# In the second batch, four of eight heads' p·v products as six bfloat16 products each, p split in place in the scores' PSUM bank

## The chip, the cores and the metric

The kernel runs on one core of a Trainium2 chip. The metric is the device time of one execution in microseconds (us). Engines are named as the profile names them: PE is TensorE's matmul, PEld its weight load, DVE is VectorE, ACT is ScalarE, POOL is GpSimd, and SP is SyncE, whose queue issues nearly all DMAs.

## The reference

Four batches, eight heads, 768 positions, head size 40. A recurrence with exponential gates (an mLSTM cell) gives each position a vector per head. The heads side by side are x, 768 x 320, and a token mixer and a channel mixer follow, with residuals:

```python
for t in range(S):
    m_new = np.maximum(f_gate[:, :, t] + m, i_gate[:, :, t])
    f_stab = np.exp(f_gate[:, :, t] + m - m_new)
    i_stab = np.exp(i_gate[:, :, t] - m_new)
    C = f_stab * C + i_stab * einsum('bhd,bhe->bhde', vt, kt)
    n = f_stab * n + i_stab * kt
    h_tilde = einsum('bhde,bhe->bhd', C, qt)
    denom = np.maximum(np.abs(einsum('bhd,bhd->bh', n, qt)), 1.0)
    y[:, :, t] = sigmoid(o_gate) * h_tilde / denom
...
h = relu(x.T @ w_tok1) @ w_tok2;  u = x + h.T
out = u + relu(u @ w_ch1) @ w_ch2
```

## The kernel before, in words

**Units.** The recurrence is computed in chunks: each batch has six units of 128 positions, (b, 0) to (b, 5). For a unit PE makes the scores k·q of the eight heads into two PSUM banks of four heads each (`st_s`, line 312, tile `ps_sc`). DVE multiplies each bank by the decay factors `dd` (`st_p`, line 322) and writes p over `dd` in SBUF. PE multiplies p with v, to which a column of ones is added that gives the denominator (`st_pv`, line 430: 41 columns a head, into the bank `po`). What comes from earlier units is added through a state C (`st_state`: q times C at line 371, the update at lines 379 to 388).

**What a unit needs beforehand.** For the unit after the current one ("n1"), POOL masks `dd` (line 283), ACT takes its exponentials in two groups of four heads (line 293, `prep_exp`) and that of `pq` (line 273), DVE multiplies `q3t` by it (line 279), and POOL scales k (`kw`, line 302). Behind p·v, ACT copies `po` out (`ht`, line 441), POOL multiplies by the sigmoid gate (line 449), DVE makes the denominator (lines 455 to 459), x (line 493) and its rounded part `xh` (line 498), and POOL the rest `xl` (line 500).

**Number formats.** Batches 0 and 1 multiply p and v in float32. Batches 2 and 3 take p and v as three bfloat16 pieces each (`st_pv3`, line 401). The mixers use a high and a low float32r part.

**Order.** There is no planner: each engine runs its instructions in the order in which the code issues them, and waits by semaphores. `att(b)` is a generator of five steps a unit: scores and loads; state; exponentials of n1; p·v and x; the second half of the exponentials and the load of n1's successor's k and v (`kvt`, line 246). The whole attention of batch 1 runs inside the channel mixer of batch 0: its last slots n = 11 to 17 each issue one `gemm1` (line 760, into `ps_h`, with `gh` on ACT, line 765, and `gl` on DVE, line 766) and one `gemm2` (line 679, into `acc`, and line 781 adds the finished sum to x), and advance `att(1)` in between by `STEPS0`. SP issues the loads in the same order: of a unit's loads, `q3t` and `pq` (lines 257 and 265) come a step ahead of `kvt` (line 246), then `dd` and `raw`.

**Buffers that matter.** `kvt` (324 KB a load) has two buffers, `ps_sc` two banks (both are one unit's), the pool `ps_m` two banks, shared by `po`, `pu` and, for the second third of batch 0's channel mixer, its two `acc` sums.

Of the kernel before, what the change touches and what calls it, by code (L numbers as in the profile page):

```python
# [7 lines left out]
F32 = mybir.dt.float32  # L8
# [3 lines left out]
BF16 = mybir.dt.bfloat16  # L12
AF = mybir.ActivationFunctionType
ALU = mybir.AluOpType
# [3 lines left out]
B, H, S, D = 4, 8, 768, 40  # L18
L = 128
NC = S // L  # L20
E1 = D + 1
DM = H * D
# [6 lines left out]
ROW = [h % 3 * 3 + h // 3 for h in range(H)]  # L29
# [5 lines left out]
def kernel(ctx: ExitStack, tc: tile.TileContext, gates, qk, q3, kv, og,  # L35
                            wt1, wt2, wc1, wc2, ident, out):
    nc = tc.nc
# [248 lines left out]
    def prep_exp(u, hf):  # L286
        b, c = u
        dd = T[u]["dd"]
        if b == 0:
            nc.scalar.activation(dd[:, 4 * hf:4 * hf + 4, :], T[u]["phi"][hf], AF.Exp)  # L290
            return
        for h in range(4 * hf, 4 * hf + 4):
            nc.scalar.activation(dd[:, h, :], dd[:, h, :], AF.Exp, bias=bcol[:, c, HP * b + h:HP * b + h + 1])  # L293
# [21 lines left out]

    def st_p(u, mid=iter(())):
        t = T[u]
        for hf in range(2):
            if hf:
                next(mid, None)  # L320
            dd = t["dd"][:, 4 * hf:4 * hf + 4, :]
            nc.vector.tensor_tensor(dd, t["s"][hf], dd, ALU.mult)  # L322

    def three(u):
        return u[0] > 1
# [19 lines left out]
    def prep_v(u):  # L345
        t = T[u]
        vx = t["kv"][:, DM:]
        w = xpool[1].tile([128, 3, H * E1], BF16, tag="v3", name="v3", bufs=1)
        r = ap.tile([128, H * E1], F32, tag="kw", name="vr", bufs=2)
        v = nc.vector  # L350
        v.tensor_copy(w[:, 0], vx)
        v.tensor_tensor(r, vx, w[:, 0], ALU.subtract)
        v.tensor_copy(w[:, 1], r)
        v.tensor_tensor(w[:, 2], r, w[:, 1], ALU.subtract)
        t["v"] = w
# [59 lines left out]
    def st_pv(u, copy=True):  # L415
        b, c = u
        t = T[u]
        vx = t["kv"][:, DM:]
        if "p" in t:
            return st_pv3(u)  # L420
        if c:
            po = t["po"]
        else:
            t["bank"] = ps_m.tile([128, 512], F32, tag="m", name="po")
            po = t["bank"][:, 0:H * E1].rearrange("p (h e) -> p h e", e=E1)
        for h in range(H):
            o, x = po[:, h, :], vx[:, h * E1:(h + 1) * E1]
            if b == 0 and c:
                o, x = po[:, 0:h + 2:h + 1, :], x.unsqueeze(1).to_broadcast([128, 2, E1])
            nc.tensor.matmul(o, t["dd"][:, ROW[h], :], x, start=c == 0 and h == 0, stop=h == H - 1)  # L430
        if b == 0 and c:
            po = po[:, 1:1 + H]
        t["po"] = po
        if b:
            st_ht(u)
# [81 lines left out]
    def att(b):  # L517
        for c in range(NC):
            u = (b, c)
            n1, n2 = after(u, 1), after(u, 2)  # L520
            th = three(u)
            if b + 1 < B and c in (3, 4):
                load_sig(b + 1, c - 3)
            if b > 1 and c == 0:
                sigmoid(b)
            st_s(u)
            if n2 and not three(u):
                load_phi(n2)
            if n1 and not three(u):
                prep_mask(n1)  # L530
            if n2:
                load_qk(n2, 0)
            if th:
                prep_p2(u)
            yield
            if th:
                prep_p3(u)
            else:
                st_state(u)
            if n1 and three(u):  # L540
                prep_mask(n1)
            yield
            if n1:
                prep_exp(n1, 0)
                if not three(n1):
                    prep_q3(n1)
                    prep_kw(n1)
            if n2:
                load_qk(n2, 1)
                if not th:  # L550
                    load_q3(n2)
            yield
            st_pv(u)
            st_hs(u)
            if not th:
                st_x(u)
            yield
            if n1 and three(n1):
                prep_v(n1)
            if th:  # L560
                st_x(u)
            if n1:
                if three(n1):
                    prep_q3(n1)
                    prep_kw(n1)
                prep_exp(n1, 1)
            if n2:
                load_kv(n2)
                if th:
                    load_q3(n2)  # L570
                    load_phi(n2)
            yield
# [212 lines left out]
    def step(g, n=1):  # L785
        for _ in range(n):
            next(g, None)
# [148 lines left out]
    for b in range(B):  # L936
# [61 lines left out]
        for n, (k, p) in enumerate(slots):  # L998
            if b == 0 and 2 < n < 11:
                step(dec_ops(9), 9)  # L1000
            g = gemm1(b, k, p, 0 if b or k == 2 else 1 if n < 2 else 2 - 2 * k)
            if b == 0:
                if n < 3:
                    dec_hi()
                    dec_abs(nxt[2] + 2, both=True)
                    dec_low()
                    step(dec_ops(9, whole=True), 9)
                if n == 2:
                    for _ in range(2):
                        dec_hi(1)  # L1010
                        dec_abs(nxt[1] + 1)
                    dec_low()
                if n == 10:
                    split_x(0, 4)
                    split_x(0, 5)
                if n == 11:
                    phase_t(0, 4, ss)
                    phase_t(0, 5, ss)
                    gemm2(*pend)
                    pend = None  # L1020
                    wx[0].release()
                    wq.release()
                    xpool[1] = ctx.enter_context(tc.tile_pool(name="xp", bufs=1, side="right"))
                    step(ag)
                if n < 11:
                    if n > 2:
                        dec_abs(nxt[2] + 2)
                        dec_hi()
                        dec_low()
                    if n > 8:  # L1030
                        sigmoid(1, (n - 9,))
                    if n in (0, 4, 6, 7, 8):
                        step(pf)
# [68 lines left out]
```

## Time and profile before

| what | value |
|---|---|
| three timed runs | 433.81 us median (433.14 to 434.11) |
| the profiled execution | 433.04 us, its span 431.3 us |
| PE busy in the span | 424.0 us (98%) |
| PEld, DVE, ACT, POOL busy | 407.1, 292.6, 185.0, 141.8 us |
| granted TensorE clock | full in all 40 slices |
| batch 1's attention | 102 to 148 us of the span |

Busy times of different engines lie beside each other. The span is what the profiler sees; the execution's own time is 1.7 us more. In rows of a timeline the first number is the start and the second the length of the instruction or run of instructions, in us; [..] at the end is idle time of the engine just before, and whom it waited for.

### The profile page before, as it was taken

How to read it: one execution, taken by the hardware profiler on the slowest of the kernel's cores; microseconds unless marked ns; L12 is line 12 of the kernel's file. 1: busy time of each engine (PE TensorE's matmuls, PEld its weight loads, DVE VectorE, ACT ScalarE, POOL GpSimd, SP SyncE). 2: the span in 40 equal slices, each digit the busy share in tenths (PEclk: the TensorE clock that was granted, in tenths of full speed). 3: DMA queues.
4: the chain of work that ended last, by engine and by line, in shares of the span. 5: the costliest groups of instructions: out<-in, count | busy, mean ns of one | idle time of the engine just before them, and what ended most of it. 6: DMA issues, size and time to landing. Idle time of an engine off the chain costs nothing.

```text
span 431.3 us, 9384 instructions
## 1 busy us (share of the span) xinstructions
PE 424.0 (98%) x3696; PEld 407.1 (94%) x3697; DVE 292.6 (68%) x650; ACT 185.0 (43%) x426; POOL 141.8 (33%) x186
## 2 busy tenths in 40 slices
PE   7999999999999999999999999999999999999996
PEld 3888999999999999999999999999999999999996
DVE  7989877745776788688795688688885645323212
ACT  5987666894544725324414336234334112211111
POOL 7487485860553410341330330331440110000000
PEclk9999999999999999999999999999999999999999
DMA  7997759813878612145356121343240000000000
GB/s 211 287 278 241 247 143 340 251 37 112 236 209 231 205 56 83 64 130 151 92 172 193 59 70 32 127 129 105 90 114 32 2 17 15 2 32 0 26 7 30
DMA packets 24576, 52.37 MB, mean 121 GB/s; under 512 B 2565, under 2 KB 13325, under 8 KB 24533
## 3 DMA queue, kind: packets, MB, share of 16 engines
q1 hardware_dynamic: 24293, 51.61, 39.1%
q8 instruction: 29, 0.48, 0.5%
q10 hardware_dynamic: 240, 0.18, 0.2%
q14 instruction: 14, 0.11, 0.1%
HBM read 47.73 MB, written 4.04 MB: 120 GB/s over the span
## 4 chain that ended last, share of the span: by engine, by line
PE 86%; DMA 5%; POOL 2%; DVE 2%; ACT 2%; issue 1%; SPq 0%; POOLq 0%; ACTq 0%
PE ps_h L760 30%; PE acc L679 28%; PE ps_a L679 5%; PE ps_sc L312 5%; PE ps_b L679 5%; PE po L430 4%; PE po L401 3%; PE pu L379 3%; DMA wst<-in_wt_dram 2%; DMA wst<-in_wc_dram 2%; PE po L407 2%; PE po L371 1%; DMA kvt<-in_kv_dram 1%; POOL c1l L673 1%; PE ps_t L741 1%
## 5 line engine op out<-in xcount | busy, mean ns | idle before, releaser
L760 PE MATMUL ps_h<-uT,c1h 128*128 128x256 f32 x720 | 137.8, 283 | 0.2
L765 ACT ACTIVATE gh<-ps_h 128x512 fp32r<-128x512 f32 x72 | 43.0, 597 | 177.9 <-PE ps_h L760 177.7
L760 PEld LDWEIGHTS ps_h<-uT,c1h 128*128 128x128 f32 x720 | 114.0, 188 | 1.4 <-DVE uT L743 0.6
L766 DVE SCALAR_TENSOR_TENSOR gl<-ps_h,gh 128x512 fp32r<-128x512 f32 x72 | 49.7, 690 | 90.3 <-ACT gh L765 90.1
L760 PE MATMUL ps_h<-uT,c1l 128*128 128x256 f32 x432 | 108.5, 281 | 0.1
L679 PE MATMUL acc<-c2h,gh 128*128 128x320 f32 x288 | 90.1, 320 | 0.0
L679 PE MATMUL acc<-c2l,gh 128*128 128x320 f32 x288 | 86.8, 309 | 0.0
L760 PEld LDWEIGHTS ps_h<-uT,c1l 128*128 128x128 f32 x432 | 79.7, 188 | 0.4 <-POOL c1l L673 0.3
L679 PE MATMUL acc<-c2h,gl 128*128 128x320 f32 x288 | 65.7, 309 | 0.1
L679 PEld LDWEIGHTS acc<-c2h,gh 128*128 128x128 f32 x288 | 54.1, 188 | 1.6
L679 PEld LDWEIGHTS acc<-c2l,gh 128*128 128x128 f32 x288 | 54.2, 188 | 0.0
L679 PEld LDWEIGHTS acc<-c2h,gl 128*128 128x128 f32 x288 | 48.1, 187 | 0.5 <-DVE gl L766 0.5
L293 ACT ACTIVATE dd<-dd,bcol 128x128 f32<-128x128 f32 x144 | 45.8, 394 | 3.5 <-POOL dd L283 3.5
L449 POOL TENSOR_TENSOR sig<-sig,ht 128x320 f32<-128x320 f32 x18 | 14.7, 816 | 96.7 <-DVE ht L411 89.2
L500 POOL TENSOR_TENSOR xl<-x,xh 128x320 fp32r<-128x320 f32 x18 | 15.8, 878 | 55.6 <-DVE xh L498 50.3
L322 DVE TENSOR_TENSOR dd<-ps_sc,dd 128x512 f32<-128x512 f32 x48 | 30.9, 681 | 1.9 <-PE ps_sc L312 1.9
L312 PE MATMUL ps_sc<-raw 64*128 64x128 f32 (+1 forms) x384 | 28.1, 285 | 0.0
L312 PEld LDWEIGHTS ps_sc<-raw 64*128 64x128 f32 (+1 forms) x384 | 23.5, 187 | 4.1 <-issue 1.9
L283 POOL TENSOR_SCALAR_AFFINE_SELECT dd<-dd 128x1024 f32<-128x1024 f32 x18 | 21.4, 1189 | 9.0 <-DMA dd<-phi_d 9.0
L430 PE MATMUL po<-kvt,dd 128*128 128x41 f32 (+1 forms) x192 | 23.3, 278 | 0.2 <-DVE dd L322 0.2
L430 PEld LDWEIGHTS po<-kvt,dd 128*128 128x128 f32 x192 | 22.5, 192 | 0.4 <-DVE dd L322 0.3
L335 DVE TENSOR_TENSOR r<-dd 128x512 f32<-128x512 f32 x24 | 22.0, 956 | 0.0
(147 smaller groups left out, 742.1 us busy)
## 6 DMA issues: line engine op xcount, KB each, us to landing
dd<-phi_d SPq DMA_DIRECT2D x18, 512.0 KB
wst<-in_wc_dram SPq DMA_DIRECT2D x22, 384.0 KB
kvt<-in_kv_dram SPq DMA_DIRECT2D x24, 324.0 KB
raw<-in_qk_dram SPq DMA_DIRECT2D x48, 160.0 KB
sig<-in_og_dram SPq DMA_DIRECT2D x8, 480.0 KB
out_dram<-x SPq DMA_DIRECT2D x24, 160.0 KB
q3t<-in_q_dram SPq DMA_DIRECT2D x20, 180.0 KB
wst<-in_wt_dram SPq DMA_DIRECT2D x8, 384.0 KB
```

Source lines behind the costliest of these rows:

```text
L283: nc.gpsimd.affine_select(dd, dd, pattern=[[0, H], [1, L]], compare_op=ALU.is_ge, fill=-1e30, base=0, channel_multiplier=-1)
L293: nc.scalar.activation(dd[:, h, :], dd[:, h, :], AF.Exp, bias=bcol[:, c, HP * b + h:HP * b + h + 1])
L312: nc.tensor.matmul(t["s"][hf][:, h, :], r[:, 1, h, :], r[:, 0, h, :], start=True, stop=True)
L322: nc.vector.tensor_tensor(dd, t["s"][hf], dd, ALU.mult)
L335: nc.vector.tensor_tensor(r[:, h], dd[:, h], top(dd)[:, h], ALU.subtract)
L430: nc.tensor.matmul(o, t["dd"][:, ROW[h], :], x, start=c == 0 and h == 0, stop=h == H - 1)
L449: nc.gpsimd.tensor_tensor(sg, sg, ht[:, :, 0:D], ALU.mult)
L500: nc.gpsimd.tensor_tensor(xl, x, f32(xh), ALU.subtract)
L679: nc.tensor.matmul(ps, a, m, start=(first and i == 0), stop=(last and i == n - 1))
L760: nc.tensor.matmul(ps[:, j, :], c1[x][:, a:a + 128], u[:, y, :], start=part is first and i == 0 and (order == 0 or j == 0), stop=i == len( ...
L765: nc.scalar.activation(gh, ps, AF.Relu)
L766: nc.vector.scalar_tensor_tensor(gl, ps, 0.0, f32(gh), op0=ALU.max, op1=ALU.subtract)
```

## The change

Only batch 1 is touched. Its eight heads are split: heads 2, 4, 5 and 7, whose p lies in the second score bank, are multiplied with v in float32 as before. Heads 0, 1, 3 and 6, those of the first bank, are multiplied as six products of bfloat16 pieces.

- p's pieces (`st_p_half`): DVE writes scores times `dd` back into the score bank; ACT copies it to bfloat16 (p1); DVE subtracts p1 in the bank; ACT copies the rest (p2); DVE subtracts p2 into a third piece. p1 and p2 take the place of the first four heads' `dd`. DVE's multiplication for the second bank stands between the first and the second of its steps.
- v's pieces (`half_v`), for four heads, in two steps: two ACT copies and two POOL subtractions in the step of the exponentials, ahead of n1's `pq`; one ACT copy and one POOL subtraction at the end of the step of `prep_exp(n1, 1)`.
- `st_pv`: four float32 products, then 24 bfloat16 products of 41 columns, each with its weight load.
- `v3` has two buffers in place of one.

```diff
     def st_p(u, mid=iter(())):
         t = T[u]
+        if u[0] == 1:
+            return st_p_half(u)
...
+    def st_p_half(u):
+        t = T[u]
+        dd, s = t["dd"], t["s"][0]
+        p12 = dd[:, 0:4].rearrange("p h t -> p (h t)").bitcast(BF16).rearrange("p (i h t) -> p i h t", i=2, h=4)
+        p3 = xpool[1].tile([128, H, L], BF16, tag="p3", name="rp", bufs=1)[:, 0:4]
+        nc.vector.tensor_tensor(s, s, dd[:, 0:4], ALU.mult)
+        nc.scalar.activation(p12[:, 0], s, AF.Copy)
+        nc.vector.tensor_tensor(dd[:, 4:8], t["s"][1], dd[:, 4:8], ALU.mult)
+        nc.vector.tensor_tensor(s, s, p12[:, 0], ALU.subtract)
+        nc.scalar.activation(p12[:, 1], s, AF.Copy)
+        nc.vector.tensor_tensor(p3, s, p12[:, 1], ALU.subtract)
+        t["half"] = (p12[:, 0], p12[:, 1], p3)
+
+    def half_v(u):
...
+        for i, x in enumerate((a, z)):
+            nc.scalar.activation(f(v[0], i), x, AF.Copy)
+        for i, x in enumerate((a, z)):
+            nc.gpsimd.tensor_tensor(f(r, i), x, f(v[0], i), ALU.subtract)
+        t["v"] = v
+        yield
+        nc.scalar.activation(v[1], r, AF.Copy)
+        nc.gpsimd.tensor_tensor(v[2], r, v[1], ALU.subtract)
+        yield
...
-        for h in range(H):
+        for h in (2, 4, 5, 7) if b else range(H):
...
+        for i, j in ((0, 0), (0, 1), (0, 2), (1, 0), (1, 1), (2, 0)) if b else ():
+            for n, h in enumerate((0, 1, 3, 6)):
+                nc.tensor.matmul(po[:, h, :], t["half"][i][:, ROW[h], :], t["v"][j][:, n * E1:(n + 1) * E1],
+                                 start=False, stop=h == 6 and i == 2)
...
+            hv = half_v(n1) if n1 and not three(n1) else iter(())
             if n1:
                 prep_exp(n1, 0)
+                step(hv)
                 if not three(n1):
                     prep_q3(n1)
                     prep_kw(n1)
...
                 prep_exp(n1, 1)
+                step(hv)
...
                     xpool[1] = ctx.enter_context(tc.tile_pool(name="xp", bufs=1, side="right"))
+                    step(half_v(units[NC]), 2)
                     step(ag)
```

DVE's queue from unit 3's scores on, before (line 322 is p, 766 the mixer's `gl`, 384 and 388 the state, 279 `q3t`, 455 the first denominator step):

```order
177 L322 TENSOR_TENSOR dd<-ps_sc,dd 128x512 x2
178 L766 SCALAR_TENSOR_TENSOR gl<-ps_h_1908,gh 128x512
179 L384 TENSOR_TENSOR pu<-pu,bm_t 120x246
180 L384 TENSOR_TENSOR pu<-pu,bm_t 80x82
181 L388 SCALAR_TENSOR_TENSOR Cn<-Cn,decay,pu 120x123 x2
182 L388 SCALAR_TENSOR_TENSOR Cn<-Cn,decay,pu 80x82
183 L279 TENSOR_TENSOR q3t<-q3t,pq 120x384
184 L455 TENSOR_SCALAR den<-ht 128x8
```

The same place of DVE's queue now (line 331 is p in the bank, 333 the second bank's p, 334 and 336 the subtractions; the other lines are the former ones moved down):

```order
186 L331 TENSOR_TENSOR ps_sc<-ps_sc,dd 128x512
187 L333 TENSOR_TENSOR dd<-ps_sc,dd 128x512
188 L334 TENSOR_TENSOR ps_sc<-ps_sc,dd 128x512
189 L336 TENSOR_TENSOR rp<-ps_sc,dd 128x512
190 L809 SCALAR_TENSOR_TENSOR gl<-ps_h_2016,gh 128x512
191 L420 TENSOR_TENSOR pu<-pu,bm_t 120x246
192 L420 TENSOR_TENSOR pu<-pu,bm_t 80x82
193 L424 SCALAR_TENSOR_TENSOR Cn<-Cn,decay,pu 120x123 x2
194 L424 SCALAR_TENSOR_TENSOR Cn<-Cn,decay,pu 80x82
195 L279 TENSOR_TENSOR q3t<-q3t,pq 120x384
196 L495 TENSOR_SCALAR den<-ht 128x8
```

Two multiplications have become four instructions, two of which wait for ACT; what was behind them is still behind them.

ACT's queue around unit 4, before (line 765 is the mixer's `gh`, 293 unit 5's exponentials, 273 unit 5's `pq`, 441 unit 4's `ht`):

```order
131 L765 ACTIVATE gh<-ps_h_2017 128x512
132 L293 ACTIVATE dd<-dd,bcol 128x128 x4
133 L273 ACTIVATE pq<-pq 120x384
134 L441 ACTIVATE ht<-po 128x328
135 L293 ACTIVATE dd<-dd,bcol 128x128 x4
```

The same place now (lines 332 and 335 make p1 and p2 of unit 4, lines 351 and 356 the pieces of unit 5's v):

```order
149 L332 ACTIVATE dd<-ps_sc 128x512
150 L335 ACTIVATE dd<-ps_sc 128x512
151 L808 ACTIVATE gh<-ps_h_2157 128x512
152 L293 ACTIVATE dd<-dd,bcol 128x128 x4
153 L351 ACTIVATE v_2202<-kvt 128x82 x2
154 L273 ACTIVATE pq<-pq 120x384
155 L481 ACTIVATE ht<-po 128x328
156 L293 ACTIVATE dd<-dd,bcol 128x128 x4
157 L356 ACTIVATE v_2202<-v_2202 128x164
```

The two copies from `kvt` stand ahead of `pq` and `ht`, and p1 and p2 ahead of `gh`.

## Rows read from the trace of the kernel before

**Rows 1.** Windows, whole stage: stretch, us, PE busy (instructions), clock, DMA share, GB/s.
```profile
104.00:148.20 44.20, 44.14 (x394) 1.00 0.77 220
```

**Rows 2.** Windows, lines 430 and 401 alone, with PEld busy behind PE.
```profile
122.10:123.84 1.74, 1.74 (x16) 1.74 (x16) 1.00 0.48 157
...
166.35:167.37 1.02, 1.02 (x32) 1.02 (x32) 1.00 0.00 0
```

**Rows 3.** Timeline of PE: p·v of units 1 to 5, and what follows.
```profile
113.25 1.88 PE L430 MATMUL po<-kvt,dd 128*128 128x41 f32 x16
...
122.10 1.92 PE L430 MATMUL po<-kvt,dd 128*128 128x41 f32 x16
123.84 0.39 PE L679 MATMUL acc<-c2h,gh 128*128 128x320 f32 x1
124.07 0.31 PE L679 MATMUL acc<-c2l,gh 128*128 128x320 f32 x1
...
129.22 1.92 PE L430 MATMUL po<-kvt,dd 128*128 128x41 f32 x16
...
138.10 1.91 PE L430 MATMUL po<-kvt,dd 128*128 128x41 f32 x16
...
144.62 1.92 PE L430 MATMUL po<-kvt,dd 128*128 128x41 f32 x16
```

**Rows 4.** Groups by line and shape: busy us, mean ns of one, idle before.
```profile
L765 ACT ACTIVATE gh<-ps_h 128x512 fp32r<-128x512 f32 x72 | 43.0, 597 | 177.9 <-PE ps_h L760 177.7
L322 DVE TENSOR_TENSOR dd<-ps_sc,dd 128x512 f32<-128x512 f32 x48 | 30.9, 681 | 1.9 <-PE ps_sc L312 1.9
L467 DVE TENSOR_TENSOR po<-po,sig 128x320 f32<-128x320 f32 x6 | 3.0, 492 | 0.3 <-PE po L430 0.2
L410 ACT ACTIVATE ht<-po 128x82 f32<-128x82 f32 x12 | 2.8, 231 | 0.0
```

**Rows 5.** Timeline of DVE, units 0 to 5.
```profile
102.50 1.29 DVE L322 TENSOR_TENSOR dd<-ps_sc,dd 128x512 f32<-128x512 f32 x2 [0.59 <-PE ps_sc L312]
...
111.45 1.28 DVE L322 TENSOR_TENSOR dd<-ps_sc,dd 128x512 f32<-128x512 f32 x2
...
126.57 1.28 DVE L322 TENSOR_TENSOR dd<-ps_sc,dd 128x512 f32<-128x512 f32 x2
128.82 0.69 DVE L766 SCALAR_TENSOR_TENSOR gl<-ps_h,gh 128x512 fp32r<-128x512 f32 x1 [0.96 <-ACT gh L765]
...
131.70 0.34 DVE L455 TENSOR_SCALAR den<-ht 128x8 f32<-128x8 f32 x1 [0.27 <-ACT ht L441]
...
133.92 1.28 DVE L322 TENSOR_TENSOR dd<-ps_sc,dd 128x512 f32<-128x512 f32 x2
...
140.25 0.56 DVE L279 TENSOR_TENSOR q3t<-q3t,pq 120x384 f32<-120x384 f32 x1 [0.41 <-ACT pq L273]
140.72 0.78 DVE L455 TENSOR_SCALAR den<-ht 128x8 f32<-128x8 f32 x1
...
142.82 1.28 DVE L322 TENSOR_TENSOR dd<-ps_sc,dd 128x512 f32<-128x512 f32 x2
```

**Rows 6.** Timeline of ACT, the exponential of unit 5's `pq`.
```profile
139.69 0.53 ACT L273 ACTIVATE pq<-pq 120x384 f32<-120x384 f32 x1 [1.75 <-DMA pq<-phi_d]
```

**Rows 7.** Timeline of SP's queue: issues of unit 5's `pq` and `kvt`.
```profile
129.23 0.73 SPq L265 DMA_DIRECT2D pq<-phi_d  x1
131.20 0.36 SPq L246 DMA_DIRECT2D kvt<-in_kv_dram  x1
```

**Rows 8.** Timeline of POOL, beside DVE's 140.72.
```profile
140.63 0.84 POOL L449 TENSOR_TENSOR sig<-sig,ht 128x320 f32<-128x320 f32 x1 [4.63 <-ACT ht L441]
```

**Rows 9.** Chain that ended last, around unit 0's `pu`: start, us, what.
```profile
105.23 0.69 DVE gl L766
105.92 0.41 DVE x L781
...
106.37 0.83 PE pu L379 x6
```

More of the change, by code (lines that the diff above doesn't have):

```diff
@@ L322, in st_p @@
             nc.vector.tensor_tensor(dd, t["s"][hf], dd, ALU.mult)
+    def st_p_half(u):
[11 more added lines that the diff above has]
+    def half_v(u):
+        t = T[u]
+        vx = t["kv"][:, DM:]
+        w = xpool[1].tile([128, 3, H * E1], BF16, tag="v3", name="v3", bufs=2)
+        w = w.rearrange("p j e -> p (j e)")
+        n = 4 * E1
+        r = w[:, 3 * n:5 * n].bitcast(F32)
+        v = [w[:, j * n:(j + 1) * n] for j in range(3)]
+        a, z = (vx[:, i:i + 4 * E1].rearrange("p (h e) -> p h e", e=E1) for i in (0, 3 * E1))
+        a, z = a[:, 0:2], z[:, 0:4:3]
+        f = lambda x, i: x.rearrange("p (h e) -> p h e", e=E1)[:, 2 * i:2 * i + 2]
+        for i, x in enumerate((a, z)):
[7 more added lines that the diff above has]
+        yield
     def three(u):
@@ L347, in prep_v @@
         vx = t["kv"][:, DM:]
-        w = xpool[1].tile([128, 3, H * E1], BF16, tag="v3", name="v3", bufs=1)
+        w = xpool[1].tile([128, 3, H * E1], BF16, tag="v3", name="v3", bufs=2)
         r = ap.tile([128, H * E1], F32, tag="kw", name="vr", bufs=2)
@@ L429, in st_pv @@
                 o, x = po[:, 0:h + 2:h + 1, :], x.unsqueeze(1).to_broadcast([128, 2, E1])
-            nc.tensor.matmul(o, t["dd"][:, ROW[h], :], x, start=c == 0 and h == 0, stop=h == H - 1)
+            nc.tensor.matmul(o, t["dd"][:, ROW[h], :], x, start=c == 0 and h == 2 * b, stop=b == 0 and h == H - 1)
+        for i, j in ((0, 0), (0, 1), (0, 2), (1, 0), (1, 1), (2, 0)) if b else ():
+            for n, h in enumerate((0, 1, 3, 6)):
+                nc.tensor.matmul(po[:, h, :], t["half"][i][:, ROW[h], :], t["v"][j][:, n * E1:(n + 1) * E1],
+                                 start=False, stop=h == 6 and i == 2)
         if b == 0 and c:
```

## The prediction

> **What bounds the kernel now.** Read first the windows of the stage in which batch 1's attention runs: PE is busy for 44.14 of 44.20 us at the full clock, and the DMA engines for 0.77 of the time [rows 1]. So whatever PE is spared here the execution gains, and whatever PE waits here it loses: nothing later catches it up, since PE is 98% busy over the whole span. The second view is the timeline of PE beside that of DVE. For each unit call S the start of DVE's first multiplication (line 322) and E the time at which PE comes to p·v (line 430). The reader is to see how close S lies to E: 111.45 and 113.25 in unit 1, 126.57 and 129.22 in unit 3, 142.82 and 144.62 in unit 5 [rows 3, 5]. That is 1.80, 2.65 and 1.80 us, for two multiplications that take 1.28 us. PE doesn't wait in any of them, but there is 0.5 us to spare in units 1 and 5. The third view is DVE's queue between two S, the fourth the loads ahead of unit 5.
>
> **What PE saves.** Eight float32 heads take 1.74 us [rows 2], so four that go take 0.87. The 24 bfloat16 products of 41 columns don't occur alone. In batches 2 and 3, 32 products, half of 41 and half of 82 columns, take 1.02 us with their weight loads [rows 2]. Were all equally long, one would take 0.032 us; were they as long as their columns, one of 41 would take 0.021. I take 0.027, between the two: 24 x 0.027 = 0.65 us (0.50 to 0.77). A unit saves 0.22 us (0.10 to 0.37), six units 1.3 (0.6 to 2.2). What a float32r product pays directly behind a bfloat16 one no row shows; behind float32 the first lasts 0.39 us against 0.31 for the next [rows 3], so 0 to 0.08 us a unit more may be gained. I take 0, and keep the 0.5 us for the range.
>
> The row and a rule of the skill differ here. The rows say 0.032 us at most for a weight load and a product. The Trainium skill's page "TensorE: Matmul & The Clock Gate", section "Back-to-back issue gap", gives about 81 ns a product for a stream of such pairs at 128 columns. By it the products would take 24 x 0.081 = 1.94 us, and PE alone would lose 1.07 us a unit, 6.4 in all. The trace has this very kind of pair, so the trace decides, and the rule gets no share of the chances.
>
> **What p's pieces take.** The chain is multiplication, copy, subtraction, copy, subtraction, over 512 elements each. A multiplication with a PSUM operand takes 0.68 us and an ACT pass out of PSUM 0.60 [rows 4]. The subtractions are not shown; they are of the same shape and engine, and writing back into a bank costs nothing extra (line 467 does so: 0.49 us for 320 elements [rows 4], less than 0.68 as its elements are fewer). I take 0.68 (0.6 to 0.75). The sum is 3 x 0.68 + 2 x 0.60 = 3.24, with hand-overs 3.35 us (3.0 to 3.5). The second bank is ready at S + 1.28 as before, since its multiplication lies beside ACT's first copy. PE first does the four float32 heads (0.87 us), then 20 products (0.54), then the four that need p3. So p3 is needed at E + 1.41, it is there at S + 3.35, and PE waits S - E + 1.94 us where that is above zero: S has to lie 1.94 us ahead of E, where 1.28 was enough.
>
> **Where S comes to lie.** DVE's queue is in order. From `gl` of unit 3 at 128.82 to the next S at 133.92 are 5.10 us, 0.27 of them idle [rows 5], so 4.83 of work. Before, DVE idled 0.96 us ahead of `gl`, for ACT. Now `gl` stands behind the third piece, at about S + 3.3, and ACT's `gh` is ready then, as it stands behind p2. One turn of DVE's queue is 3.3 + 4.8 = 8.1 us. PE's turn is (144.62 - 113.25) / 4 = 7.84 us on average [rows 3]. DVE's chain thus becomes longer than PE's turn, and S falls back.
>
> - Unit 0: here S is early (102.50 [rows 5]), and nothing waits for p. But behind it stand `gl` and line 781, and PE's `pu` waits for the bank that line 781 empties: 105.23, 105.92, 106.37 [rows 9]. Now `gl` can start at 102.50 + 3.3 = 105.8 rather than 105.23: PE loses 0.5 us. It gains 0.22 in its p·v: it is 0.28 late.
> - Unit 1: S = 111.65 (0.2 late, since `ht` comes that much later), E = 113.25 + 0.28 = 113.53, a wait of 0.1. PE is 0.16 late.
> - Unit 2: S = 119.75, E = 122.26, none. PE is 0.06 early.
> - Unit 3: S = 127.85, E = 129.16, a wait of 0.63. PE is 0.35 late.
> - Unit 4: S = 135.95, E = 138.45, none. PE is 0.13 late.
> - Unit 5: S would be 144.05 by DVE's turn. A load makes it later. ACT's `pq` waited for its DMA until 139.69 [rows 6]. The two new copies from `kvt` stand ahead of it, and `kvt` was issued 2 us behind `pq` on the same queue [rows 7]. Its 324 KB at the stage's 220 GB/s [rows 1] are 1.5 us, so it lands at 139.7 to 141.2. I take 140.9, nearer the later end, as unit 0's delay puts off that queue too. Two copies of 0.23 us [rows 4], overlapping, end at 141.3. `pq` starts 1.6 us late, and S, which lay 2.57 us behind `q3t` (140.25 to 142.82 [rows 5]), comes to 144.45. E = 144.75, a wait of 1.64 us, 1.0 of it already at the float32 heads, because the second bank's p is ready only at 145.73.
>
> The waits are 0.5 + 0.1 + 0.63 + 1.64 = 2.9 us, less 1.3 saved: +1.6 us. The profiled execution took 433.04 us, which would become 434.6. It lies 0.77 below the median of the timed runs, so the forecast for these is 433.81 + 1.6 = 435.4. With the chain at 3.0 or 3.5 us, the saving at its ends, and `kvt` at either end, the sum runs from +0.6 to +2.7.
>
> What costs nothing: the third piece of v on POOL and its ACT copy fall in POOL's and ACT's idle time (ACT's was 1.75 us ahead of `pq`, POOL's 4.63 ahead of line 449, in unit 5's preparation [rows 6, 8]), and v is needed only at E + 0.87. If that cover went, PE would wait for them as for p3. The second `v3` buffer adds no wait.
>
> **The rivals.** *POOL and DVE block each other (more slower).* Line 455 takes 0.34 us at 131.70 and 0.78 at 140.72, where it ends together with POOL's line 449 (140.63 to 141.47) [rows 5, 8]. The three new POOL instructions a unit, up to 0.8 us, stand around the time of `q3t` and the denominator. If DVE stands still for 0.4 us of them, its turn is 8.5 us: S in units 3 and 5 is 128.65 and 145.65, the waits are 0.5, 0.1, 1.4 and 2.0, and the sum +2.8: 436.6; with 0.8 us it is about +4.3: 438.1. Against it speaks that three of the four DVE instructions of the new chain have a PSUM operand. The Trainium skill's page "SBUF — State Buffer", section "SBUF: two separate sides", says that the two engines share a port pair which one holds for a whole instruction, a VectorE one with two SBUF inputs among them. By it `q3t`, x and the second denominator step could be held, p's steps not; the 0.78 us row agrees as to the holding.
>
> *Waits and saving cancel (no change).* If `kvt` lands with `pq`, put off by 0.4 us only, and DVE's work between two S shrinks by 0.3 us, unit 3 doesn't wait; in unit 5 S is 143.2 and E 144.15, a wait of 1.0. The sum is 0.5 + 0.1 + 1.0 - 1.3 = +0.3: 434.1.
>
> *The chain is covered (faster).* The place is DVE's turn: it decides as soon as it lies below PE's 7.84 us by more than the first turn's delay. If the holding above goes away where it is now (0.78 against 0.34 us, 0.44 of it), the turn is 7.66 us, S keeps its distance, and with `kvt` landing with `pq` the waits are 0.5, 0.1 and 0.4: with the saving at 1.3 us the sum is -0.3, with 2.2 us it is -1.2, 432.6, and with the change of format 432.1. For it speaks that DVE has idle time to give up, 0.96 us ahead of `gl`, which the sum uses up already; against it that S - E is too small in units 1 and 5 from the start.
>
> **How the numbers follow.** The forecast gets 0.53, the blocking rival 0.24, no change 0.15, faster 0.08. A measurement of this kernel tells 0.2%, 0.87 us, from no change. The forecast's own range is 434.4 to 436.5. The range for 8 in 10 reaches half-way into no change below and to the milder blocking and somewhat beyond above: 434.2 to 437.6. Slower by over 0.2% (above 434.68) are most of the forecast and the blocking rival, 0.76; within it 0.16; faster 0.08.
>
> **What would show it right or wrong.** In the changed profile: 24 products in 0.5 to 0.8 us a unit; DVE's first multiplication and the third piece 3.0 to 3.5 us apart; DVE's turns of about 8 us in units 1 to 4; waits of PE at unit 0's `pu` for line 781's successor, and in units 3 and 5 for p, unit 5's the longest; ACT's copies of unit 5's v waiting for `kvt`. Behind batch 1 all stages should have the length of before. The forecast is wrong if PE doesn't wait in unit 5, if S keeps its distance to E, or if p's pieces take 4 us or more.

## The result and the profile after

The changed kernel took 436.45 us (median of six runs, 435.69 to 438.30), the kernel before on the same chip 433.48 (six runs, 432.73 to 434.11). The ratio is 1.0076, with a 95% interval from 1.0053 to 1.0099: 2.3 to 4.3 us slower. The forecast was 435.4 us, 1.6 us slower. Its range held the time, but the loss of 1.6 us itself lies below that interval. The profiled execution took 437.03 us, its span is 435.3.

PE's timeline, up to its last product, has three parts: up to unit 0's scores 101.31 us before and 102.20 after, from there to the first product of batch 1's token mixer (`ps_a`), "the stage" from here on, 46.89 and 49.97, and the rest 279.83 and 279.80. So nothing is lost behind the stage; 3.08 us are lost in it, and 0.9 ahead of it, where PE's clock was 0.50 from 8 to 11 us in this execution and full before. That part lies between 100.88 and 104.94 us in the kernels below, whatever the edit, so the stage is what is compared.

Windows of the stage, and of the stretch in which the clock fell (us, busy time of PE, PEld, DVE, ACT, POOL, then the granted clock, DMA share, GB/s; the first row answers to [rows 1]):

```profile
104.93:152.20 47.27, 45.12 (x490) 42.53 (x489) 38.37 (x84) 31.48 (x92) 24.71 (x39) 0.96 0.75 214
130.00:134.00 4.00, 3.30 (x45) 2.94 (x44) 3.20 (x6) 2.59 (x7) 2.34 (x3) 1.00 0.88 240
134.00:137.00 3.00, 3.00 (x22) 2.44 (x20) 2.90 (x8) 2.71 (x10) 2.50 (x5) 0.51 0.88 260
```

PE now stands for 2.15 us that the profile shows as idle. And for 3 us, behind a stretch in which it was busy for 3.30 of 4 us, its granted clock is 0.51, the lower of its two levels (1.2 GHz). PE's timeline around p·v in units 0 to 3 and 5 (start, length, [idle before, releaser]; line 466 the float32 products, 469 those of pieces; answers to [rows 3]):

```profile
107.94 0.83 PE L415 MATMUL pu<-kvt,kw 128*120 128x123 f32 x6 [0.73 <-DVE x L824]
...
114.52 1.04 PE L466 MATMUL po<-kvt,dd 128*128 128x41 f32 x8
115.39 0.92 PE L469 MATMUL po<-v,dd 128*128 128x41 bf16 x20
116.66 0.27 PE L469 MATMUL po<-v,rp 128*128 128x41 bf16 x4 [0.36 <-DVE rp L336]
116.78 0.39 PE L722 MATMUL acc<-c2h,gh 128*128 128x320 f32 x1
...
123.92 1.02 PE L466 MATMUL po<-kvt,dd 128*128 128x41 f32 x8
124.78 0.67 PE L469 MATMUL po<-v,dd 128*128 128x41 bf16 x20
125.29 0.26 PE L469 MATMUL po<-v,rp 128*128 128x41 bf16 x4
125.39 0.39 PE L722 MATMUL acc<-c2h,gh 128*128 128x320 f32 x1
...
131.20 1.09 PE L466 MATMUL po<-kvt,dd 128*128 128x41 f32 x8 [0.26 <-DVE dd L333]
132.11 0.92 PE L469 MATMUL po<-v,dd 128*128 128x41 bf16 x20
133.39 0.27 PE L469 MATMUL po<-v,rp 128*128 128x41 bf16 x4 [0.35 <-DVE rp L336]
...
134.93 2.08 PE L312 MATMUL ps_sc<-raw 64*128 64x128 f32 x16
...
144.68 1.16 PE L312 MATMUL ps_sc<-raw 64*128 64x128 f32 x16
...
150.22 0.27 PE L469 MATMUL po<-v,rp 128*128 128x41 bf16 x4 [0.29 <-DVE rp L336]
```

Unit 2 waits for nothing: its p·v takes 125.39 - 123.92 = 1.47 us, against 1.74 [rows 2]. Unit 1's takes 116.78 - 114.52 = 2.26. So it loses 0.79 us, though its rows show an idle time of 0.36 only: the products that need p2 wait in their weight loads before (PEld idles 0.18 us at 115.93 for p2, and 0.46 at 116.66 for the third piece), and the run of 20 hides it. The scores take 2.08 us at 134.93 and 1.16 at 144.68; that is the clock.

One whole turn of DVE's queue, from unit 1's S to unit 2's (331 to 336 the steps of p, 420 and 424 the state, 809 `gl`, 495 to 499 the denominator; answers to [rows 5]):

```profile
113.13 0.69 DVE L331 TENSOR_TENSOR ps_sc<-ps_sc,dd 128x512 f32<-128x512 f32 x1
113.73 0.68 DVE L333 TENSOR_TENSOR dd<-ps_sc,dd 128x512 f32<-128x512 f32 x1
114.55 0.70 DVE L334 TENSOR_TENSOR ps_sc<-ps_sc,dd 128x512 f32<-128x512 f32 x1
115.91 0.69 DVE L336 TENSOR_TENSOR rp<-ps_sc,dd 128x512 bf16<-128x512 f32 x1 [0.66 <-ACT dd L335]
116.52 0.69 DVE L420 TENSOR_TENSOR pu<-pu,bm_t 120x246 f32<-120x246 f32 x2
...
117.97 0.68 DVE L809 SCALAR_TENSOR_TENSOR gl<-ps_h,gh 128x512 fp32r<-128x512 f32 x1
118.57 0.55 DVE L279 TENSOR_TENSOR q3t<-q3t,pq 120x384 f32<-120x384 f32 x1
119.04 0.16 DVE L495 TENSOR_SCALAR den<-ht 128x8 f32<-128x8 f32 x1
119.23 0.58 DVE L497 SCALAR_TENSOR_TENSOR den<-ht,den 128x8 f32<-128x8 f32 x1
...
120.60 0.49 DVE L533 TENSOR_TENSOR x<-sig,den 128x320 f32<-128x320 f32 x1 [0.55 <-POOL sig L489]
121.12 0.33 DVE L538 CAST xh<-x 128x320 fp32r<-128x320 f32 x1
121.37 0.69 DVE L331 TENSOR_TENSOR ps_sc<-ps_sc,dd 128x512 f32<-128x512 f32 x1
```

The turn is 8.24 us; the later ones are 8.49, 8.48 and 8.35 (S at 129.86, 138.34, 146.69). DVE idles twice, for p2 and for `sig`. Call the chain of work that leads from one unit's S to the next one's a ring: DVE's own queue is one, and `sig` is the end of a second, through ACT and POOL. POOL in the same turn:

```profile
117.77 0.64 POOL L353 TENSOR_TENSOR v<-kvt,v 128x82 f32<-128x82 f32 x2 [2.11 <-ACT v L351]
118.35 0.19 POOL L278 COPY decay<-pq 120x3 f32<-120x3 f32 x1
118.50 1.29 POOL L302 TENSOR_TENSOR kw<-kvt,wcol 128x320 f32<-128x320 f32 x1
119.75 0.81 POOL L489 TENSOR_TENSOR sig<-sig,ht 128x320 f32<-128x320 f32 x1
```

`kw` starts 5.37 us behind S here, and 5.02 in the same turn without v's pieces (e2, below); and it takes 1.29 us, beside DVE's `q3t` and denominator, where it takes 0.72 at 110.51. In the two longest turns DVE doesn't idle for `sig`, but its lines 495 and 497 take 0.70 and about 0.74 us beside `kw` and `sig` (at 127.27 and 128.01). In other turns of these kernels each takes as little as 0.16 or 0.17. So both rings are slower than PE's turn of 7.84 us, and they touch each other.

The steps of p by group (busy us, mean ns of one, idle before; answers to [rows 4]), and ACT ahead of unit 5 (351 the copies of v; answers to [rows 6]):

```profile
L334 DVE TENSOR_TENSOR ps_sc<-ps_sc,dd 128x512 f32<-128x512 f32 x6 | 4.2, 700 | 0.7
...
L331 DVE TENSOR_TENSOR ps_sc<-ps_sc,dd 128x512 f32<-128x512 f32 x6 | 4.2, 693 | 0.6 <-PE ps_sc L312 0.6
L336 DVE TENSOR_TENSOR rp<-ps_sc,dd 128x512 bf16<-128x512 f32 x6 | 4.1, 692 | 4.0 <-ACT dd L335 4.0
```

```profile
142.63 0.42 ACT L351 ACTIVATE v<-kvt 128x82 bf16<-128x82 f32 x2
142.95 0.51 ACT L273 ACTIVATE pq<-pq 120x384 f32<-120x384 f32 x1
```

All six third pieces together leave DVE idle for 4.0 us, waiting for p2. In unit 5 neither the copies of v nor `pq` waited for a load: ACT came to the copies at 142.63, while before it had stood waiting for `pq` until 139.69; `kvt` had landed by then.

### The profile page after: what moved, and what is told of

Its sections match the earlier page's. It is cut to its first block, busy times and chain, and to the rows that moved or that the text cites. A ratio compares the mean times of both kernels' runs of the same rounds, so it can differ in the third digit from the quotient of the medians.

```text
span 435.3 us, 9641 instructions
## 1 busy us (share of the span) xinstructions
PE 425.1 (98%) x3792; PEld 407.9 (94%) x3793; DVE 300.3 (69%) x662; ACT 193.7 (44%) x456; POOL 149.3 (34%) x204
## 4 chain that ended last, share of the span: by engine, by line
PE 81%; DVE 6%; POOL 5%; ACT 3%; DMA 3%; issue 2%; POOLq 0%; ACTq 0%; DVEq 0%; SPq 0%
PE ps_h L803 27%; PE acc L722 26%; PE ps_a L722 5%; PE ps_sc L312 5%; PE ps_b L722 5%; PE po L437 3%; PE po L466 2%; PE pu L415 2%; DMA wst<-in_wc_dram 2%; PE po L443 2%; DVE ps_sc L334 1%; DVE ps_sc L331 1%; PE po L407 1%; PE ps_phi L179 1%; POOL kw L302 1%
## 5 line engine op out<-in xcount | busy, mean ns | idle before, releaser
L312 PE MATMUL ps_sc<-raw 64*128 64x128 f32 (+1 forms) x384 | 29.6, 296 | 0.0
L312 PEld LDWEIGHTS ps_sc<-raw 64*128 64x128 f32 (+1 forms) x384 | 24.9, 198 | 4.2 <-issue 2.5
L324 DVE TENSOR_TENSOR dd<-ps_sc,dd 128x512 f32<-128x512 f32 x36 | 23.3, 681 | 1.1 <-PE ps_sc L312 1.1
L700 DVE SCALAR_TENSOR_TENSOR pf<-pf,wst 128x384 int32<-128x384 int32 x30 | 16.2, 559 | 7.6 <-ACT wst L678 3.3
L371 DVE TENSOR_TENSOR r<-dd 128x512 f32<-128x512 f32 x24 | 20.8, 905 | 0.0
L302 POOL TENSOR_TENSOR kw<-kvt,wcol 128x320 f32<-128x320 f32 x20 | 18.5, 925 | 2.2 <-ACT wcol L141 2.2
```

Source lines behind the costliest of these rows:

```text
L302: nc.gpsimd.tensor_tensor(kw, t["kv"][:, 0:DM].rearrange("p (h d) -> p h d", d=D), wcol[:, c, HP * b:HP * b + H].unsqueeze(2).to_broadcast ...
L312: nc.tensor.matmul(t["s"][hf][:, h, :], r[:, 1, h, :], r[:, 0, h, :], start=True, stop=True)
L371: nc.vector.tensor_tensor(r[:, h], dd[:, h], top(dd)[:, h], ALU.subtract)
L700: v.scalar_tensor_tensor(fi, fi, 3, raw[:, :, 0], op0=ALU.logical_shift_left, op1=ALU.bitwise_or)
```

## The experiments

The length of each unit, in us from scores to scores on PE (unit 5's to `ps_a`), in the profiled execution of each kernel. A star marks a unit with a stretch at the lower clock. The ratio is to the kernel before, run beside it.

| kernel | 0 | 1 | 2 | 3 | 4 | 5 | stage | median us | ratio (95%) |
|---|---|---|---|---|---|---|---|---|---|
| before | 7.58 | 8.00 | 8.01 | 7.12 | 8.87 | 7.30 | 46.89 | 433.48 | |
| changed | 7.95 | 8.56 | 7.73 | 8.48* | 9.75* | 7.50 | 49.97 | 436.45 | 1.0076 (1.0053 to 1.0099) |
| e1 products only | 7.29 | 7.73 | 7.74 | 6.85 | 8.63 | 7.93 | 46.16 | 432.41 | 0.9983 (0.9960 to 1.0006) |
| e2 no v pieces | 7.95 | 8.22 | 7.74 | 7.76 | 8.62 | 8.57 | 48.87 | 436.13 | 1.0061 (1.0036 to 1.0087) |
| e3 no p pieces | 7.28 | 7.95 | 7.73 | 6.85 | 8.62 | 8.84 | 47.28 | 435.06 | 1.0034 (1.0013 to 1.0056) |
| e5 units 0, 2, 4 | 7.34 | 8.00 | 7.73 | 7.13 | 9.71 | 7.69 | 47.60 | 433.11 | 0.9995 (0.9976 to 1.0014) |
| e4 unit 0's tail late | 7.35 | 8.90 | 7.73 | 8.38 | 8.62 | 10.38* | 51.35 | 436.74 | 1.0074 (1.0046 to 1.0103) |
| e7 q3t on POOL | 7.95 | 8.83 | 7.75 | 8.64 | 8.63 | 10.17* | 51.97 | 438.67 | 1.0114 (1.0082 to 1.0146) |
| e10 no p, v late | 7.28 | 7.90 | 7.73 | 6.89 | 8.62 | 9.65* | 48.08 | 434.16 | 1.0004 (0.9972 to 1.0036) |
| e12 gl in the gap | 7.95 | 8.56 | 7.73 | 7.11 | 8.61 | 10.19* | 50.15 | 436.35 | 1.0061 (1.0032 to 1.0090) |
| e13 v behind sig | 7.95 | 8.32 | 7.73 | 7.94 | 8.62 | 10.13* | 50.70 | 436.66 | 1.0071 (1.0041 to 1.0101) |
| e11 both rings | 7.35 | 8.71 | 7.73 | 7.00 | 8.62 | 7.81 | 47.23 | 433.83 | 1.0007 (0.9980 to 1.0034) |
| e8 units 0, 2, 4, v late | 7.35 | 8.00 | 7.73 | 7.13 | 8.62 | 7.32 | 46.15 | 431.96 | 0.9971 (0.9941 to 1.0002) |
| e14 the same again | 7.35 | 8.00 | 7.73 | 7.13 | 8.62 | 7.41 | 46.24 | 432.26 | 0.9965 (0.9945 to 0.9985) |

A unit without waits is shorter by 0.24 to 0.29 us (e1, units 0 to 4), 1.6 in all six. What a unit has above e1's length (7.03 in unit 5, 7.30 less 0.27) is wait or clock. The changed kernel has 0.66 + 0.83 + 0 + 1.63 + 1.12 + 0.47 = 4.7 us of it. Of that about 1.5 is the clock: 1.12 in unit 4, and in unit 3 the 0.37 that its waits (0.42 ahead of p·v, 0.84 in it) leave over. Waits: 3.2.

**e1, products alone.** The six products a head read bits of `dd` and `kvt` that lie there already; neither p's nor v's pieces are made:

```diff
-        if u[0] == 1:
-            return st_p_half(u)
...
-                nc.tensor.matmul(po[:, h, :], t["half"][i][:, ROW[h], :], t["v"][j][:, n * E1:(n + 1) * E1],
+                nc.tensor.matmul(po[:, h, :], top(t["dd"])[:, ROW[h], :], top(vx)[:, h * E1:(h + 1) * E1],
```

> Four float32 heads as before and 24 bfloat16 products of 41 columns a unit, but p's and v's pieces are left out: all 24 read the upper halves of the float32 p and v, so the values are not the reference's. This is TensorE's part of the change alone. Theory A (the waits come from the longer chain of p's pieces in VectorE's queue): without the chain only the saving is left, 0.27 us a unit by the changed trace (1.47 us from the first float32 product of unit 2 to the next accumulator product, 1.74 before), -1.6 us in all. Theory B (v's pieces on GpSimd and ScalarE make the waits): the same -1.6. Theory C (the bfloat16 products themselves, their weight loads or the clock, cost time): 0 or slower than before.

The stage is 0.73 us shorter, less than half of the 1.6 expected. Five units gain in full; unit 5 gives 0.9 back. There ACT's `pq` waits for its load:

```profile
142.41 0.52 ACT L273 ACTIVATE pq<-pq 120x384 f32<-120x384 f32 x1 [2.15 <-DMA pq<-phi_d]
```

PE comes earlier to unit 5, the load does not, and S depends on it. So even without any pieces to make, the gain ends at the load of unit 5.

**e2, no pieces of v** (the second operand as in e1, p's pieces in full):

> p's pieces as in the change; v's pieces are left out, the products read the upper half of the float32 v. Theory A: VectorE still needs its chain of 3.4 us, the time between two first multiplications falls only from 8.4 to about 8.1 us, and the kernel stays slower than before by 1.5 to 2.5 us. Theory B: with GpSimd's three subtractions and ScalarE's three copies gone GpSimd no longer holds VectorE, the time between two first multiplications falls to 7.8 us or less, and the kernel is at -0.5 to +0.5 us of before.

1.98 us are lost in the stage at the full clock, in the changed kernel's places: 0.66 in unit 0, 0.49, 0.91 and 1.54 in units 1, 3 and 5. DVE's turns are 8.17 to 8.22 us, and between unit 1's S and unit 2's DVE idles only in the 0.66 us ahead of the third piece. p's chain makes DVE's ring too long without any pieces of v, beside the work that POOL had before: in the turns from unit 1 to unit 4 `q3t` takes 0.72 to 0.78 us and line 495 0.77 or 0.78, beside `kw` and `sig`, against 0.55 and 0.16 in the fence above.

**e3, no pieces of p** (the first operand as in e1, v's pieces in full):

> v's pieces are made as in the change, p is multiplied as before and the products read the upper half of the float32 p; p's pieces are left out. Theory A: no chain, so nearly the whole saving shows, -1.0 to -1.6 us. Theory B: GpSimd still holds VectorE and ScalarE still copies v ahead of pq, so p comes late in units 3 and 5 and the kernel is at 0 to +2 us.

No wait at `pu`; unit 5 loses 1.81 us. ACT's two copies of v stand waiting for `kvt`, with `pq` behind them:

```profile
140.68 0.43 ACT L349 ACTIVATE v<-kvt 128x82 bf16<-128x82 f32 x2 [1.40 <-DMA kvt<-in_kv_dram]
141.02 0.51 ACT L273 ACTIVATE pq<-pq 120x384 f32<-120x384 f32 x1
```

Counted from unit 0's scores, `pq` starts 39.43 us behind them here and 38.30 in e1, 1.1 us later. The prediction had put `pq` off by 1.6 us here: 1.2 until `kvt` lands, 0.4 for the copies. Of the 1.81 us, e1 has 0.90 without any pieces.

**e4, unit 0's tail late.** p2 and the third piece of unit 0 are issued behind slot 12's `gl` and additions:

```diff
                     gemm2(*pend, half=1)
                     pend = None
+                    if n == 12:
+                        next(T[units[NC]]["tail"], None)
```

> The changed kernel, with one thing moved: of unit 0's chain the second subtraction, the copy p2 and the third piece are issued behind gl and line 824's addition (x) of the mixer's slot 12, so that PE's pu no longer waits behind them (0.73 us in the changed kernel). Theory A (DVE's queue as a whole is the bound: its turn of 8.2 to 8.5 us sets every S from unit 1 on): the wait at pu goes, but DVE has the same work before S of unit 1, so PE, 0.7 us earlier, waits about as much more at p's pieces of units 1 to 5; the stage (scores of unit 0 to the end of batch 1) is shorter than the 48.9 to 50.0 us of the kernels with p's pieces by 0.3 us at most, time 435.8 to 436.4. Rival (the waits are single and independent, as the prediction added them up): the stage is 0.7 us shorter, the other waits stay at 0.35 each, time 435.5 to 435.7 or less. A wait of 0 to 0.5 us for unit 0's own third piece would count against either.

Unit 0 gains 0.60 us. Unit 1 is 0.34 us longer than in the changed kernel, unit 3 0.27 longer (without the 0.37 of clock there), and unit 5, which no clock ahead of it spares now, has 3.35 us too much, clock included. The wait moved; the time didn't fall, and the stage, which was expected a little shorter, is longer. The single waits are not terms that can be taken away one at a time.

**e7, q3t on POOL.** One expression at line 279 (`nc.gpsimd` for batch 1 too):

> The changed kernel with batch 1's q3t multiplication on POOL instead of DVE (0.55 us on DVE; 1.02 us on POOL, where the other batches have it). Theory A (DVE's queue is the bound): DVE's turn between two first multiplications falls from 8.2 to 8.5 to about 7.8 us, PE's own turn, and the waits for the third piece in units 3 and 5 shrink below 0.2 us or go; the stage is 1.0 to 1.5 us shorter than the changed kernel's (49.97 us, of which a half-clock stretch made some), time 434.5 to 435.3. Rival P (POOL's new work holds DVE at their shared port): POOL now holds DVE longer, kw takes 1.2 us or more still, DVE's turn stays above 8.2 us, time 436 or more. Rival C (the products themselves cost more than they save): no change of the waits matters, 436.4.

DVE is relieved by 0.55 us a turn, and its turn grows to 8.63 or 8.64 us three times running. POOL in the turn from unit 1 to 2:

```profile
119.25 0.64 POOL L353 TENSOR_TENSOR v<-kvt,v 128x82 f32<-128x82 f32 x2 [2.11 <-ACT v L351]
119.84 0.18 POOL L278 COPY decay<-pq 120x3 f32<-120x3 f32 x1
119.98 1.00 POOL L279 TENSOR_TENSOR q3t<-q3t,pq 120x384 f32<-120x384 f32 x1
120.94 0.72 POOL L302 TENSOR_TENSOR kw<-kvt,wcol 128x320 f32<-128x320 f32 x1
121.63 0.82 POOL L489 TENSOR_TENSOR sig<-sig,ht 128x320 f32<-128x320 f32 x1
```

POOL is busy without a gap up to `sig`, and x follows at 122.48. Line 495 takes 0.90 us beside it, so DVE gets little of its relief; but DVE then still idles 0.55 us for `sig`, so its queue isn't what ends last. So the theory "DVE's queue alone is the bound" fell. `kw` takes 0.72 us here, so it isn't `kw`'s holding up either. There are two rings, and this edit lengthened the second: p2, `gh`, exponentials, copies of v, v's subtractions, `q3t`, `kw`, `sig`, x, S.

**e12, gl in the gap.** p2 and the third piece are issued behind `gh` and `gl` (from unit 2 on), which takes `gl` out of DVE's ring and `gh` out of the other:

```diff
+            t["tail"] = g = st_p_half(u)
+            next(g)
...
         nc.vector.tensor_tensor(s, s, p12[:, 0], ALU.subtract)
+        yield
...
+            if c > 1:
+                next(t.get("tail", iter(())), None)
```

> The changed kernel with only one thing moved: from unit 2 on p2 and the third piece are issued behind the mixer's gh and gl (in unit 1 the third piece behind the state's first step), so that gl fills the 0.66 us in which DVE waits for p2, and gh stands ahead of p2 on ACT. Unit 0 and v's pieces are as in the changed kernel. Theory R: DVE's ring becomes 7.6 us and that through ACT and POOL, which loses gh's 0.5 us, 7.7 to 7.9; the waits at pu (0.73) and in unit 1 (0.35) stay, those in units 3 and 5 for the third piece shrink to 0.2 or less, unit 5 may wait 0.5 to 1.6 us for its loads; stage 47.3 to 48.6 us, time 434.2 to 435.4. Rival (DVE's queue isn't what is late): turns of 8.2 us or more as before the move, stage 48.9 or more, time 436.

DVE's turn from unit 2 to 3 is 7.71 us, and unit 3 waits 0.26 in place of 0.9 or more. But unit 5 is 3.2 us too long: ACT's copies of v waited 1.23 us for `kvt`, ahead of `pq`, and the clock fell. R's turn came true, its time (434.2 to 435.4) didn't.

**e13, v's first step behind sig:**

```diff
-                step(hv)
...
             st_hs(u)
+            step(hv)
```

> The changed kernel with only one thing moved: the first step of v's pieces is issued behind sig (on ACT behind ht, on POOL behind sig's multiplication) instead of ahead of pq and kw. Theory R: the ring through ACT and POOL loses about 1 us, but DVE's own ring stays at 8.17 us as in the run without v's pieces, so the waits stay (0.7 at pu, 0.33 to 0.36 at the third piece of units 1, 3 and 5, up to 0.6 more in unit 5) and the stage is 48.6 to 49.1 us, time 435.6 to 436.3. Rival (v's place decides, as it did in the run with units 0, 2 and 4): turns below 7.9 us, stage 47.5 or less, time 434 or less.

Three turns are 8.26 or 8.27 us (R: 8.17), and in them DVE idles only for p2, 0.66 us each; the time is the changed kernel's. The stage is longer than expected by unit 5, 3.1 us too long with its clock.

**e10, no pieces of p, v late** (e3 with v's first step behind `pq`, `q3t` and `kw`):

> No pieces of p are made (the products read the bits of dd in their place, so that the values of the four heads are not the reference's); v's pieces are made in full, their first step behind pq, q3t and kw. With that step ahead of pq the stage took 47.28 us, 0.39 more than before, all by a wait of 1.61 us in unit 5. Theory K (that wait is kvt's: ACT's copies stood waiting for its DMA ahead of pq): ACT's pq of unit 5 starts when its own DMA lands, the wait falls to the 0.7 us of the run with the products alone, the stage to 46.0 to 46.5 us, time 432.2 to 432.7. Rival (POOL's and ACT's work on v delays p by itself, wherever it stands): the stage stays at 47.0 to 47.5 us, time 433.5 to 435.

A miss for K's numbers: unit 5 still loses 1.5 us and then the clock. `pq` no longer waits behind `kvt`, but the copies still stand ahead of `ht`, and held it by 0.65 us for `kvt`; x and S come behind `ht`. The median, 434.16, doesn't tell the two expectations apart, the rows do. (The five of its ten executions whose mean granted clock is 0.999 or more have a median of 432.53, where K expected 432.2 to 432.7.)

**e11, both rings** (e4, e12 and e13 together, full work in six units):

> All six units with split products, and the two rings that seem to set the turn both shortened. Theory R: the turn of 8.2 to 8.6 us comes from two rings of nearly the same length. One is DVE's own queue (8.17 us without v's pieces, of which 0.66 us is idle time for p2). The other goes through ACT and POOL: p2, gh, exponentials, copies of v, pq, then on POOL v's subtractions, kw and sig, then x and the next S. Here p2 and the third piece are issued behind the mixer's gh and gl (in unit 1 behind the first state step), so that gl fills the 0.66 us, v's first step stands behind sig, and unit 0's tail behind the additions of slot 12. R expects DVE's turn at 7.5 to 7.7 us, no wait of PE at pu or in units 1 to 4, at most 0.7 us in unit 5 (as in the run of the products alone), the stage at 45.6 to 46.3 us (before: 46.89), time 431.9 to 432.6. Rival L (the loads of unit 5, pq and kvt, take back whatever is gained): a wait of 1.5 us or more in unit 5, stage 46.8 us or more, time 433.3 or more. Rival D (DVE's subtractions and multiplications take longer beside POOL's work, wherever they stand): turns of 8 us or more, 434.5 or more.

The turns fall to 7.77 to 7.87 us (0.2 above what was expected), and `pu` costs 0.06. Of the changed kernel's 4.7 us 2.0 are left, 0.98 in unit 1 and 0.78 in unit 5, and they eat the 1.6 saved: 1.0007. A miss for R's time. Unit 1 waits because its S follows unit 0's by 9.29 us: in that turn DVE idles 0.87 us for `pq` and 0.54 for `sig`, so it isn't DVE's work that sets it. It is ACT's: unit 0's p2 (to 109.37) still stands ahead of a table load of 1.28 us (at 109.39), the exponentials and `pq`.

**e5, e8 and e14, units 0, 2 and 4 only.** e5 has `st_p_half` and `half_v` for these three units, and unit 0's tail late; e8 moves v's first step:

```diff
-                step(hv)
                 if not three(n1):
                     prep_q3(n1)
                     prep_kw(n1)
+                step(hv)
```

> The change in units 0, 2 and 4 alone, those in which TensorE comes to p times v 3.6 us or more after the first multiplication could start; units 1, 3 and 5 in float32 as before. In unit 0 the second copy and the third piece are issued behind the mixer's gl and the sums added to x. Theory A: the chain fits into the room of these units, and VectorE's idle time makes up for it before units 1, 3 and 5 (1.28 us ahead of TensorE is enough there): three savings of 0.27 us and no wait, -0.4 to -0.8 us. Theory B: three units of v's pieces make half of the waits, +0.5 to +1. Theory C: half of the cost, +1 to +1.5.

> The split products in units 0, 2 and 4 only (433.11 us, stage 47.60 against 46.89 before; unit 0's tail late as in the run named e4_u0_late), and now the first step of v's pieces stands behind pq, q3t and kw instead of ahead of them. Theory K (the copies from kvt held pq in unit 4's preparation, ACT waited there 2.25 us for kvt's DMA): the wait of 0.35 us at unit 4's third piece goes and unit 4's S comes 0.5 us or more earlier; the stage falls to 46.2 to 47.0 us, time 432.3 to 432.9, a little faster than before. Rival A (DVE's chain alone makes unit 4 late): waits as without the move, stage 47.4 to 47.8, time 433.0 to 433.3.

> The kernel of the run e8_024_v_late once more, with more rounds: split products in units 0, 2 and 4 only, v's first step behind pq, q3t and kw, unit 0's tail late. It took 431.96 us, 0.9971 of before with 1.0002 as the upper end. Theory R: three units save 0.25 us each and nothing waits, a ratio of 0.9980 to 0.9985 (432.6 to 432.9 against 433.4), the upper end below 1. Rival: the first measurement was chance, the ratio is 0.9995 or more.

In e5 unit 4 loses 1.08 us, with ACT's copies of v waiting 2.25 us for `kvt` ahead of `pq`. In e8 that is gone. The stage of e14:

```profile
104.00:148.00 44.00, 43.88 (x445) 42.20 (x444) 33.25 (x79) 27.67 (x78) 21.59 (x30) 1.00 0.75 226
```

PE is busy for all but 0.12 us. The units with the long chain alternate with units that need only two multiplications, and S catches up in these. 0.9965 (0.9945 to 0.9985): it beats both kernels. Its stage is shorter by 0.65 us, the low end of that interval. The rest fits the clock of the kernel it is compared with: 12 of the 35 executions of the kernel before, run beside it, have a mean granted clock of 0.996 or less, but only one of e14's twelve. The medians of the others are 432.96 (23 executions) and 432.26 us (eleven), 0.70 us apart.

## Why the prediction was right, and where it was not

The direction and the mechanism were right: p's chain makes DVE's turn longer than PE's, S falls back, and PE waits at unit 0's `pu` and in units 1, 3 and 5, not in 2 and 4. By its own steps:

- *What PE saves.* 0.22 us a unit was forecast, 0.24 to 0.29 measured (e1). Right; the rows of batches 2 and 3 were a good price.
- *The chain.* 3.35 us was forecast; unit 1's took 116.60 - 113.13 = 3.47. Right. Writing back into the score bank cost nothing: 0.69 to 0.70 us a step against 0.68.
- *The turn.* 8.1 us forecast, 8.24 to 8.49 measured. Too short because only DVE's instructions were added up. e2 and e13 show this ring at 8.17 to 8.27 us; the rest is the ring through ACT and POOL, which the prediction didn't have, with `kw` at 1.29 us in place of 0.72.
- *The waits in units 0, 1 and 3.* 0.5, 0.1 and 0.63 forecast; 0.66, 0.83 and 1.26 measured. The first turn is where it begins: S of unit 1 came 9.73 us behind S of unit 0, where 9.15 was forecast, and later turns add 0.1 to 0.4 each. That first turn runs through ACT, which the forecast left out: unit 0's p2 stands ahead of a table load (1.28 us), unit 1's exponentials and `pq`, and the copies of v ahead of `pq`, so that DVE idles 0.57 us for `pq`. The turn is 8.93 us in e1, 9.24 with v's pieces alone (e3), 9.41 with p's alone (e2).
- *Unit 5.* 1.64 forecast, 0.47 measured, so two signs that it named didn't show: unit 5's wait as the longest, and ACT's copies waiting for `kvt`. In this execution PE had lost so much by then that the load had landed and S had caught up. Where it had not, the forecast mechanism is there (e3: 1.81 us, 0.90 of it the load of `pq` alone as in e1; e12).
- *The step that failed* is the one that priced a wait at its own length alone. The waits summed to 3.2 us (2.9 forecast); that these sums agree is luck, since units 1 and 3 waited 1.4 us more than forecast and unit 5 1.2 less. But behind the thin stretch in unit 3 lie 3 us at the lower clock, another 1.5 us. The prediction took the full clock of before for granted. 3.2 + 1.5 - 1.6 = 3.1, the 3.08 us of the stage.

Of the rivals, *POOL and DVE block each other* was nearest in time (436.6). Its rows are there: `kw` 1.29 us. The Trainium skill's page "SBUF — State Buffer", section "SBUF: two separate sides", says that whichever of a GpSimd instruction and a VectorE one with two SBUF inputs starts first holds the shared ports for its whole length. `kw`, 0.57 us longer beside `q3t` (0.55 us), fits a hold of that length, though the rows let `kw` start 0.07 us ahead of `q3t`. But e2, without POOL's new work, is 1.0061 with turns of 8.17 to 8.22 us, so that work isn't what the loss needs: all that v's pieces add to the later turns, by holding or otherwise, is up to 0.3 us. Line 495 and `q3t` are lengthened in e2 too, by POOL's old work; how much of the loss would go if they weren't, no run shows. *Waits and saving cancel* needs the load and the turn both shorter; e11, which shortens the rings, is that case. *The chain is covered* needed DVE's turn below PE's: in e14 S keeps up with PE, because every second unit has no chain.

Only the profiled execution has rows that say where the clock fell, but the mean granted clock of every timed one is on record. It is 0.996 or less in four of the changed kernel's six, in 47 of 69 executions of e2, e3, e4, e7, e10, e12 and e13, in whose profiled executions one unit loses 1.5 us or more (clock included), in 10 of 58 of e1, e5, e8, e11 and e14, and in 24 of 96 of the kernel before beside them. So the lower clock goes with long waits, though it also comes without them, and no run changes the waits and nothing else. It isn't the whole loss: the median of e2's five executions at 0.999 or more is 435.26 us, that of the 26 of before beside them at 0.998 or more 433.35. The 1.9 us between them agree with the 1.98 of e2's stage, which had the full clock. The changed kernel has two such executions, at 435.69 and 438.30 us; what made the second so long stays open.

## What to carry to other kernels

Where one engine is bound and others feed it in a loop, add up every ring that leads from a unit's start to the next one's, through every engine that an instruction waits for, not only the busiest queue: two rings of 8.2 us made each single relief worthless (e7, e13); only a change to both shortens the turn (e11, e12). A conversion that spares the bound engine a quarter of a microsecond a unit but puts two engines' round trips ahead of it pays where alternate units leave time to catch up. And put no instruction that waits for a late load ahead of one that others wait for: unit 4 gained 1.09 us when two small copies moved behind `pq` (e5 to e8).

## What the runs showed of the hardware

- A wait can be followed by a cost beyond its length. Behind thin stretches PE's granted clock was about 0.5 for some 3 us: in the changed kernel (PE busy 3.30 of 4 us ahead of it) and at the end of e4, e7, e10, e12 and e13. Not always: e2 (3.00 of 4) and e3 (2.48 of 4) kept the full clock. In e4:

```profile
144.00:148.00 4.00, 2.48 (x23) 2.36 (x21) 3.31 (x9) 1.72 (x6) 2.14 (x4) 1.00 0.78 216
...
150.00:152.00 2.00, 2.00 (x11) 2.00 (x12) 1.28 (x3) 2.00 (x8) 0.81 (x1) 0.53 0.84 240
```

- PE's idle time in a timeline understates its waits. Unit 1 lost 0.79 us with 0.36 shown, since products that wait in their weight loads lie within a run that reads as busy.
- A bfloat16 product of 41 columns with its own weight load takes about 0.026 us in a stream: 20 of them start at 124.78, the next at 125.29.
